# Query, output and key-sum transposition in a fused attention and two-layer feed-forward kernel: DMA in place of TensorE

## The chip, the cores and the metric

The kernel runs on one core of one Trainium2 chip. The metric is the device time of the whole program in microseconds (us). Engines are called by the names of the profile: PE is TensorE (matmuls), DVE is VectorE, ACT is ScalarE, POOL is GpSimd, and SP is SyncE, which issues every DMA of this kernel on one queue.

## The reference, cut to what matters

```python
# q (2, 12288, 128), kv (2, 384, 32, 128); the rows of q are scaled by 8
kv_pool = kv.reshape(B, H // 4, 4, W // 4, 4, C).mean(axis=(2, 4))   # 96 x 8 = 768 keys of 128
k = v = kv_pool.reshape(B, -1, C) @ w_sr
a = softmax((q @ k.transpose(0, 2, 1)) / sqrt(C))
x = (a @ v).reshape(B * S, D)                       # 24576 tokens of 128
h = x @ w_in;  x = (h * clip(h + 3, 0, 6) / 6) @ w_out        # d_ff = 2048
h = x @ w_in2; x = (h * cos(h)) @ w_out2                      # d_ff = 2048
```

## The kernel before

The tokens go in 48 blocks of 512, 24 for each of the two batches. In a block everything stands with the features on the partitions and the tokens along the row, so queries have to be transposed on the way in and outputs on the way out.

**Keys.** `plan_kv` (one call for each batch) makes the 768 pooled keys in six chunks of 128. A chunk is 16 rows of 128 features that have to be summed: two loads bring eight of them each, in two tiles of 128 x 1024. In the first batch (at the start of the program) the chunk is halved twice by adds of one half to the other (L448, `KV_HALVINGS` = 2), and the four parts that are left are summed and transposed by four PE matmuls against the identity (L457). In the second batch (in the middle of the program, beside other work) it is halved four times, in widths of 1024, 512, 256 and 128, and one PE matmul turns the result. Every add but the first has both operands in one SBUF tile; the first may go to DVE or to POOL.

**Attention.** `plan_attention` loads the block's queries (L550), turns them with four PE transposes of 128 x 128 into a PSUM bank (L558), and splits them into a high part (ACT, L561) and a low part (DVE, L564) in a tile x. Scores are L600, row maximum L606, exponential L612, normalisation on POOL L627. The attention weights are turned by a DMA: DVE lays the upper and lower half words of every value apart (L655), SP stores them to a DRAM scratch (L662), and a transposing DMA brings them back (L698); L714 multiplies them with the values (fp32 matmuls). Blocks 0 and 1 (`BY_PE` = 2) do that on PE instead (L683).

**Feed-forward.** `plan_unit` takes 256 hidden features: six matmuls of 512 columns in (L765 to L767), the gate on ACT and DVE (L780 and L783 in layer 1; L788, L791, L797, L800 in layer 2), a high part on ACT (L827), a low part on POOL (L803), and six matmuls out (L773 to L775). A block has 8 units in each layer. `plan_store` scales the result (ACT L850 or DVE L852), turns it by four PE transposes (L860), copies it out of PSUM (L325 on ACT, L327 on DVE) and stores it (L863).

**What sets the order.** Nothing is scheduled while it runs. `Plan.run` is a list scheduler that runs when the program is written: each step has a priority (`prio`, in nanoseconds), the engines it may use with an assumed cost, the steps it waits for, and the buffers it takes and gives back (13 tiles w of 128 x 1024 fp32, 7 hi, 6 lo, 6 x, 8 PSUM banks). It writes each engine's instructions in the order that it finds, and on the chip each engine goes through its row in that order, waiting where an operand is not there. A DMA takes a w tile only where more than `SPARE` = 5 are free.

## Time and profile before

| | us |
|---|---|
| three runs before, median (lowest to highest) | 2714.81 (2714.35 to 2715.35) |
| the profiled execution, its own time | 2709.69 |
| its span, first to last instruction | 2707.6 |
| PE busy in the span | 2641.4 |
| ACT busy | 2310.1 |
| DVE busy | 2115.5 |
| POOL busy | 2010.5 |

The views used are the page's busy times, a table of busy times by stretch of the span, the waits of one engine in one stretch, the timeline of one engine (start, duration, and in brackets the idle time before and what ended it), and the groups of instructions by line. The duration of a matmul overlaps the next one's, so its price is read from the distance of starts, not from its own length. The granted clock is given as a share of the upper of TensorE's two levels (1.2 and 2.4 GHz).

### The profile page before, as it was taken

Reading aid. Unit: us, or ns where it says so; the run is one execution under the profiler, and the core shown is the slowest. Engines: PE = TensorE matmul, PEld = TensorE weight load, DVE = VectorE, ACT = ScalarE, POOL = GpSimd, SP = SyncE. Lnnn points to the kernel's source line nnn. Section 1 sums busy time; section 2 is a strip of 40 time slices with the busy share of each in tenths; the row PEclk is TensorE's granted clock in tenths of the full one; section 3 lists DMA queues with packets and bytes.
Section 4 is the critical chain, followed back from the end, with each engine's and each line's share of the span. In section 5 each row is a group of like instructions: output and inputs, shape, how many; then the busy total and the mean of one; then the engine's idle time right before and its main releaser. Section 6 shows DMA issues by size and latency. Waiting matters only on the chain. (4 is left out here: it accounts for less than half of the span.)

```text
span 2707.6 us, 32274 instructions
## 1 busy us (share of the span) xinstructions
PE 2641.4 (98%) x11504; PEld 2100.2 (78%) x11504; DVE 2115.5 (78%) x2254; ACT 2310.1 (85%) x2647; POOL 2010.5 (74%) x969
## 2 busy tenths in 40 slices
PE   6889999999999999999999999999999999999999
PEld 5667877788878877778877888788878887888787
DVE  6998777777777887787777777777777777777776
ACT  4788889898988878888888888888888888989888
POOL 1657777777777777777777777777777777777777
PEclk9999999999999999999999999999999999999999
DMA  5422223222322243322232223222322232223210
GB/s 149 132 55 63 55 78 78 63 55 73 84 63 55 82 111 81 90 59 55 72 84 63 55 72 84 62 55 68 89 62 55 73 84 63 55 72 84 55 51 12
DMA packets 387056, 192.99 MB, mean 71 GB/s; under 512 B 292560, under 2 KB 367440, under 8 KB 386896
## 3 DMA queue, kind: packets, MB, share of 16 engines
q1 hardware_dynamic: 386896, 190.95, 27.1%
q8 instruction: 90, 1.47, 0.2%
q14 instruction: 70, 0.57, 0.1%
HBM read 33.62 MB, written 84.93 MB: 44 GB/s over the span
## 5 line engine op out<-in xcount | busy, mean ns | idle before, releaser
L803 POOL TENSOR_TENSOR lo<-w,hi 128x1024 fp32r<-128x1024 f32 x768 | 1834.7, 2412 | 635.3 <-ACT hi L827 387.8
L827 ACT CAST hi<-w 128x1024 fp32r<-128x1024 f32 x768 | 787.3, 1055 | 138.3 <-DVE w L783 79.2
L765 PE MATMUL banks<-x,w_in_hi 128*128 128x512 f32 x1536 | 636.3, 414 | 17.3 <-DVE w L783 9.7
L800 DVE TENSOR_TENSOR w<-w,banks 128x1024 f32<-128x1024 f32 x384 | 463.6, 1217 | 198.9 <-ACT w L797 198.6
L773 PE MATMUL banks<-hi,w_out_hi 128*128 128x512 f32 x1536 | 610.7, 398 | 7.2 <-DVE w L783 7.2
L774 PE MATMUL banks<-hi,w_out_lo 128*128 128x512 f32 x1536 | 600.7, 391 | 3.3 <-DVE w_out_lo L399 3.3
L775 PE MATMUL banks<-lo,w_out_hi 128*128 128x512 f32 x1536 | 600.9, 391 | 1.9 <-POOL lo L803 1.9
L767 PE MATMUL banks<-x,w_in_hi 128*128 128x512 f32 x1536 | 601.3, 391 | 0.1
L766 PE MATMUL banks<-x,w_in_lo 128*128 128x512 f32 x1536 | 600.8, 391 | 0.3
L783 DVE SCALAR_TENSOR_TENSOR w<-w,banks 128x1024 f32<-128x1024 f32 x384 | 457.8, 1214 | 116.9 <-ACT w L780 116.1
L791 DVE SCALAR_TENSOR_TENSOR w<-banks,w 128x1024 f32<-128x1024 f32 x384 | 463.7, 1217 | 60.1 <-ACT w L788 58.1
L780 ACT ACTIVATE w<-banks,three 128x1024 f32<-128x1024 f32 x384 | 418.1, 1115 | 55.8 <-PE banks L767 52.6
L788 ACT ACTIVATE w<-banks 128x1024 int32<-128x1024 f32 x384 | 389.0, 1026 | 56.1 <-PE banks L767 54.8
L797 ACT ACTIVATE w<-w 128x1024 f32<-128x1024 f32 x384 | 404.4, 1067 | 35.8 <-DVE w L791 33.1
L765 PEld LDWEIGHTS banks<-x,w_in_hi 128*128 128x128 f32 x1536 | 289.2, 188 | 115.3 <-DVE w L783 21.3
L766 PEld LDWEIGHTS banks<-x,w_in_lo 128*128 128x128 f32 x1536 | 289.5, 188 | 71.1 <-issue 15.1
L773 PEld LDWEIGHTS banks<-hi,w_out_hi 128*128 128x128 f32 x1536 | 289.5, 188 | 69.0 <-DVE w L783 8.1
L774 PEld LDWEIGHTS banks<-hi,w_out_lo 128*128 128x128 f32 x1536 | 289.6, 189 | 65.1 <-DVE w_out_lo L399 4.4
L775 PEld LDWEIGHTS banks<-lo,w_out_hi 128*128 128x128 f32 x1536 | 289.2, 188 | 63.9 <-POOL lo L803 2.8
L767 PEld LDWEIGHTS banks<-x,w_in_hi 128*128 128x128 f32 x1536 | 288.9, 188 | 62.7 <-DVE x L737 0.7
L655 DVE COPY w<-w 128x1536 uint16<-128x1536 uint16 x184 | 317.1, 1744 | 5.7 <-POOL w L627 5.1
L714 PE MATMUL banks<-w,v_all 128*128 128x512 f32 x576 | 269.6, 592 | 0.0
(64 smaller groups left out, 1915.5 us busy)
## 6 DMA issues: line engine op xcount, KB each, us to landing
scr<-w SPq DMA_DIRECT2D x184, 384.0 KB, 2.5
w<-in_kv_dram SPq DMA_DIRECT2D x48, 256.0 KB, 5.1
w<-in_q_dram SPq DMA_DIRECT2D x48, 256.0 KB, 2.8
out_dram<-w SPq DMA_DIRECT2D x48, 256.0 KB, 2.0
w<-in_moe_w_in_dram SPq DMA_DIRECT2D x8, 512.0 KB, 7.5
w<-in_moe_w_out_dram SPq DMA_DIRECT2D x8, 512.0 KB, 6.7
w<-scr SPq DMA_TRANSPOSE x138, 4.6
w_sr_sb<-in_w_sr_dram SPq DMA_DIRECT2D x1, 64.0 KB, 1.8
```

The lines of the kernel that those rows point to most:

```text
L765: nc.tensor.matmul(t[:, i, :], w_hi[:, k, :], xx[:, 0, :], start=True, stop=False)
L766: nc.tensor.matmul(t[:, i, :], w_lo[:, k, :], xx[:, 0, :], start=False, stop=False)
L767: nc.tensor.matmul(t[:, i, :], w_hi[:, k, :], xx[:, 1, :], start=False, stop=True)
L773: nc.tensor.matmul(t, o_hi[:, k, :], h[:, i, :], start=(k == 0), stop=False)
L774: nc.tensor.matmul(t, o_lo[:, k, :], h[:, i, :], start=False, stop=False)
L775: nc.tensor.matmul(t, o_hi[:, k, :], l[:, i, :], start=False, stop=(k == 2 * NP - 1))
L780: nc.scalar.activation(plan[g], two(ps), AF.Relu, bias=three, scale=1.0)
L783: nc.vector.scalar_tensor_tensor(out=plan[g], in0=plan[g], scalar=6.0, in1=two(ps), op0=ALU.min, op1=ALU.mult)
L791: nc.vector.scalar_tensor_tensor(out=plan[g], in0=two(ps), scalar=0.25, in1=plan[g].bitcast(I32), op0=ALU.add, op1=ALU.subtract,)
L800: nc.vector.tensor_tensor(out=plan[g], in0=plan[g], in1=two(ps), op=ALU.mult)
L803: nc.gpsimd.tensor_tensor(out=plan[lo], in0=plan[g], in1=plan[hi].bitcast(F32), op=ALU.subtract)
L827: prio + HI_AT, {"act": 947}, lambda e: nc.scalar.copy(plan[hi], plan[g]), [a],
```

## The change

Three things change.

1. **Queries** of blocks 2 to 47: the four PE transposes and the DVE subtraction go. Instead POOL lays the half words apart (L576), SP stores them to a new scratch `scrq` (L582), a transposing DMA brings them back into the same tile (L588), ACT makes the high part from SBUF (L594), and POOL the low part (L597). The load is planned 20 us earlier (`Q_AHEAD`).
2. **Outputs** of blocks 0 to 46: the four PE transposes and the copy out of PSUM go. POOL lays the half words apart (L917), SP stores them (L923), a transposing DMA brings them back (L928), and SP stores the result (L933).
3. **Key sums**, both batches: each half chunk of 128 x 1024 is summed by one DVE reduction over its eight rows (L449) into a small tile `sum`, reading with a step of one row (512 bytes), and two PE matmuls add the two halves and turn them (L458).

```diff
-KV_HALVINGS = 2
+Q_AHEAD = 20000
...
-            def add(n):
+            def add(half):
                 def emit(e):
-                    f, f2 = (flat(plan[k]) for k in keys) if n == 0 else (flat(plan[keys[0]]),) * 2
-                    w = 1024 >> n
-                    at = w if n else 0
-                    ENG[e].tensor_tensor(
-                        out=f[:, 0:w], in0=f[:, 0:w], in1=f2[:, at : at + w], op=ALU.add
-                    )
+                    f = flat(plan[keys[half]])
+                    nc.vector.tensor_reduce(
+                        out=plan[sums][:, half, :], in_=f.rearrange("p (x c) -> p c x", c=C),
+                        axis=AX.X, op=ALU.add,
+                    )
...
-                where = {"dve": 70 + (1.6 if b else 1.04) * w}
-                if n == 0:
-                    where["pool"] = 2303
-                a = [op(prio, where, add(n), a, drop=[] if n else [keys[1]])]
-            a = op(prio, {"pe": 216 * left}, transpose, a, take=[(ps, "one")],
+                a = op(
+                    prio, {"dve": 1135}, add(half), [load(half), a],
+                    take=[] if half else [(sums, "sum")], drop=[keys[half]],
+                )
+            a = op(prio, {"pe": 432}, transpose, [a], take=[(ps, "one")], drop=[sums])
...
-        a = op(prio + Q_AT, {"pe": 436}, transpose, [a], take=[(ps, "one")], drop=[raw])
-        a = op(prio + Q_AT + 100, {"act": 478}, high, [a], take=[(qt, "x")])
-        q_op = op(prio + Q_AT + 200, {"dve": 602}, low, [a], drop=[ps])
+            at = prio - Q_AHEAD
+            a = op(at - LOAD_AHEAD, {"dma": 1000}, load, take=[(raw, "w")])
+            a = op(at, {"pool": 1250}, halves, [a], take=[(scr, "scrq")])
+            a = op(at + 1000, {"dma": 500}, away, [a])
+            a = op(at + 2000, {"dma": 1500}, back, [a], drop=[scr])
+            a = op(prio + Q_AT + 100, {"act": 478}, high_t, [a], take=[(qt, "x")])
+            q_op = op(prio + Q_AT + 200, {"pool": 1230}, low_t, [a], drop=[raw])
...
         a = op(prio, {"act": 478, "dve": 600}, scaled, [after], take=[(o, "w")], drop=[acc])
+        if b < NB - 1:
+            a = op(prio + 2000, {"pool": 1250}, halves, [a], take=[(scr, "scro")])
+            a = op(prio + 2100, {"dma": 500}, away, [a])
+            a = op(prio + 2200, {"dma": 1500}, back, [a], drop=[scr])
+            op(prio + 2300, {"dma": 1000}, store_t, [a], drop=[o])
+            return
```

The new `halves`, `away` and `back` of a query block, which those of an output block follow with other shapes:

```python
def halves(e):    # 128 x 1024 half words, read with a step of two half words
    nc.gpsimd.tensor_copy(planes.rearrange("p (j h c) -> p j h c", j=NJ, h=2),
                          words.rearrange("p (j c h) -> p j h c", j=NJ, h=2))
def away(e):      # SP, SBUF to DRAM scratch
    nc.sync.dma_start(out=plan[scr].rearrange("(j p h) c -> p j (h c)", j=NJ, h=2), in_=parted()[1]...)
def back(e):      # SP, transposing DMA, DRAM scratch to SBUF
    nc.sync.dma_start_transpose(out=parted()[0], in_=plan[scr])
```

What that makes of the engines' rows is shown at three places. First PE, late in the second batch, where an output is turned between the value matmuls of a block (L714 before, L756 after). Before:

```order
L767 MATMUL banks<-x_107,w_in_hi 128x512
L714 MATMUL banks<-w_78,v_all 128x512 x2
L860 MATMUL banks<-ident,w_88 128x128 x4
L714 MATMUL banks<-w_89,v_all 128x512 x2
L765 MATMUL banks<-x_107,w_in_hi 128x512
L766 MATMUL banks<-x_107,w_in_lo 128x512
```

At the same place after (L807 to L809 are the former L765 to L767):

```order
L809 MATMUL banks<-x_104,w_in_hi 128x512
L756 MATMUL banks<-w_88,v_all 128x512 x2
L807 MATMUL banks<-x_104,w_in_hi 128x512
L808 MATMUL banks<-x_104,w_in_lo 128x512
L809 MATMUL banks<-x_104,w_in_hi 128x512
```

The four transposes are gone from the row, and what follows a value matmul is a feed-forward matmul; the query's four (L558) are missing in the same way a few rows on.

Second SP, one block's DMAs in the second batch (scr is the scratch of the attention weights, in_q the queries). Before:

```order
L698 DMA_TRANSPOSE w_90<-scr_120 128x2x1024
L863 DMA out_dram<-w_83 128x512
L550 DMA w_86<-in_q_dram 128x512
L662 DMA scr_118<-w_78 128x3x512
L662 DMA scr_118<-w_88 128x3x512
L662 DMA scr_118<-w_82 128x3x512
L662 DMA scr_118<-w_90 128x3x512
```

After:

```order
L549 DMA w_79<-in_q_dram 128x512
L740 DMA_TRANSPOSE w_89<-scr_128 128x2x1024
L740 DMA_TRANSPOSE w_88<-scr_128 128x2x1024
L740 DMA_TRANSPOSE w_81<-scr_128 128x2x1024
L923 DMA scro_124<-w_85 128x1024
L928 DMA_TRANSPOSE w_85<-scro_124 128x4x256
L582 DMA scrq_122<-w_79 128x4x256
L933 DMA out_dram<-w_85 128x512
L588 DMA_TRANSPOSE w_79<-scrq_122 128x1024
L704 DMA scr_128<-w_82 128x3x512
```

Two DMAs of a block between the attention's transposes and its stores have become five in a row, each of which waits for the one before it of its own chain; the query load has moved ahead of the attention's transposes.

Third DVE, the first chunk of the second batch's keys. Before:

```order
L448 TENSOR_TENSOR w_90<-w_90,w_81 128x1024
L564 TENSOR_TENSOR x_104<-banks,x_104 128x512
L791 SCALAR_TENSOR_TENSOR w_82<-banks,w_82 128x1024
L448 TENSOR_TENSOR w_90<-w_90 128x512
L783 SCALAR_TENSOR_TENSOR w_78<-w_78,banks 128x1024
L800 TENSOR_TENSOR w_82<-w_82,banks 128x1024
L783 SCALAR_TENSOR_TENSOR w_88<-w_88,banks 128x1024
L448 TENSOR_TENSOR w_90<-w_90 128x256
L448 TENSOR_TENSOR w_90<-w_90 128x128
```

After (L833 and L842 are the former L791 and L800):

```order
L449 TENSOR_REDUCE sum_110<-w_88 128x128
L842 TENSOR_TENSOR w_83<-w_83,banks 128x1024
L833 SCALAR_TENSOR_TENSOR w_84<-banks,w_84 128x1024
L833 SCALAR_TENSOR_TENSOR w_87<-banks,w_87 128x1024
L842 TENSOR_TENSOR w_84<-w_84,banks 128x1024
L842 TENSOR_TENSOR w_87<-w_87,banks 128x1024
L833 SCALAR_TENSOR_TENSOR w_82<-banks,w_82 128x1024
L449 TENSOR_REDUCE sum_110<-w_90 128x128
```

Four adds whose two operands lie in SBUF have become two reductions with one operand, and the gate's steps stand between them.

## Rows read from the trace of the kernel before

**Rows 1.** The page's busy times of the engines, with their share and instruction counts.

```profile
PE 2641.4 (98%) x11504; PEld 2100.2 (78%) x11504; DVE 2115.5 (78%) x2254; ACT 2310.1 (85%) x2647; POOL 2010.5 (74%) x969
```

**Rows 2.** Busy time by stretch of the span; the first line names the columns.

```profile
core 0: us, PE busy (x) PEld busy (x) DVE busy (x) ACT busy (x) POOL busy (x), PEclk, DMA share, GB/s
0.00:57.00 57.00, 35.87 (x201) 29.58 (x202) 32.53 (x56) 20.22 (x39) 7.88 (x15) 1.00 0.63 176
57.00:212.00 155.00, 134.68 (x543) 98.63 (x541) 145.53 (x185) 124.87 (x148) 90.31 (x43) 0.98 0.30 84
212.00:940.00 728.00, 727.48 (x3180) 581.80 (x3179) 564.77 (x601) 636.29 (x725) 564.25 (x273) 1.00 0.26 67
940.00:1170.00 230.00, 211.39 (x893) 165.45 (x892) 192.85 (x182) 183.85 (x210) 164.65 (x76) 0.97 0.35 90
1170.00:2600.00 1430.00, 1429.44 (x6251) 1143.37 (x6250) 1106.86 (x1169) 1252.26 (x1428) 1097.88 (x530) 1.00 0.26 68
```

**Rows 3.** Waits of PE from 940 to 1170 us: total, times, longest.

```profile
PE banks L457 <- DVE w L448: 6.4, 2, 3.3
PE banks L773 <- DVE w L783: 5.8, 1, 5.8
```

**Rows 4.** Timeline of PE around a query's four transposes: start, duration, instruction.

```profile
1004.80 0.40 PE L775 MATMUL banks<-lo,w_out_hi 128*128 128x512 f32 x1
1005.04 0.60 PE L558 MATMUL banks<-ident,w 128*128 128x128 f32 x4
1005.39 0.48 PE L765 MATMUL banks<-x,w_in_hi 128*128 128x512 f32 x1
1005.71 0.40 PE L766 MATMUL banks<-x,w_in_lo 128*128 128x512 f32 x1
1005.94 0.40 PE L767 MATMUL banks<-x,w_in_hi 128*128 128x512 f32 x1
```

**Rows 5.** Groups by line: the PE transposes of outputs and of queries.

```profile
L860 PE MATMUL banks<-ident,w 128*128 128x128 f32 x192 | 28.8, 273 | 0.7 <-ACT w L850 0.7
L558 PE MATMUL banks<-ident,w 128*128 128x128 f32 x192 | 28.6, 272 | 1.4 <-DVE x L741 1.4
```

**Rows 6.** Timelines of DVE, POOL and PE in the second batch's key sums.

```profile
1036.71 7.35 DVE L448 TENSOR_TENSOR w<-w 128x512 f32<-128x512 f32 x3
...
1036.27 7.64 POOL L803 TENSOR_TENSOR lo<-w,hi 128x1024 fp32r<-128x1024 f32 x3 [0.66 <-ACT hi L827]
...
1045.25 0.79 PE L773 MATMUL banks<-hi,w_out_hi 128*128 128x512 f32 x1 [5.77 <-DVE w L783]
...
1172.37 0.28 DVE L448 TENSOR_TENSOR w<-w 128x128 f32<-128x128 f32 x1
```

**Rows 7.** Groups by line (count, busy us, mean ns, idle before), and one line's shortest/median/longest.

```profile
L803 POOL TENSOR_TENSOR lo<-w,hi 128x1024 fp32r<-128x1024 f32 x768 | 1834.7, 2412 | 635.3 <-ACT hi L827 387.8 <-PE banks L775 124.6 <-issue 84.5
L627 POOL TENSOR_SCALAR w<-w,s 128x768 f32<-128x768 f32 x192 | 174.6, 921 | 55.0 <-DVE s L623 48.4 <-ACT w L612 2.8 <-DMA w<-in_moe_w_out_dram 2.3
L606 DVE TENSOR_REDUCE s<-banks 128x1 f32<-128x768 f32 x192 | 179.8, 953 | 82.2 <-PE banks L600 78.9
...
L655 DVE COPY w<-w x184: 1731/1744/1756, 93.7 to 2595.4; 128x1536 uint16<-128x1536 uint16 x184
```

**Rows 8.** Timelines of DVE and PE at the first batch's last chunk of keys.

```profile
28.02 1.23 DVE L448 TENSOR_TENSOR w<-w,w 128x1024 f32<-128x1024 f32 x1 [1.97 <-DMA w<-in_kv_dram]
29.28 0.69 DVE L448 TENSOR_TENSOR w<-w 128x512 f32<-128x512 f32 x1
...
30.12 1.13 PE L457 MATMUL banks<-ident,w 128*128 128x128 f32 x8 [2.12 <-DVE w L448]
```

**Rows 9.** DMA issues by line: count, KB each, median us from issue to landing.

```profile
scr<-w SPq DMA_DIRECT2D x184, 384.0 KB, 2.5
w<-in_q_dram SPq DMA_DIRECT2D x48, 256.0 KB, 2.8
w<-scr SPq DMA_TRANSPOSE x138, 4.6
```

More of the change, by code (lines that the diff above doesn't have):

```diff
@@ L296, in attention_ffn_ffn_kernel @@
             "x": tiles("x", NX, [P, 2, T], F32R),
+            "sum": tiles("sum", 2, [P, 2, C], F32),
             "s": tiles("s", 8, [P, 4], F32),
@@ L454, in transpose @@
             def transpose(e):
-                for i in range(left):
-                    f = flat(plan[keys[i // 8]])
+                for i in range(2):
                     nc.tensor.matmul(
-                        one(ps)[:, 0:P], f[:, i % 8 * C : (i % 8 + 1) * C], ident,
-                        start=(i == 0), stop=(i == left - 1),
+                        one(ps)[:, 0:P], plan[sums][:, i, :], ident,
+                        start=(i == 0), stop=(i == 1),
                     )
@@ L567, in low, with parted, halves, turned @@
             )
-        a = op(prio - LOAD_AHEAD, {"dma": 1000}, load, take=[(raw, "w")])
-        a = op(prio + Q_AT, {"pe": 436}, transpose, [a], take=[(ps, "one")], drop=[raw])
-        a = op(prio + Q_AT + 100, {"act": 478}, high, [a], take=[(qt, "x")])
-        q_op = op(prio + Q_AT + 200, {"dve": 602}, low, [a], drop=[ps])
+        scr = ("scrq", b)
+        def parted():
+            t = flat(plan[raw]).bitcast(U16)
+            return t[:, 0 : 2 * T], t[:, 2 * T : 4 * T]
+        def halves(e):
+            words, planes = parted()
+            nc.gpsimd.tensor_copy(
+                planes.rearrange("p (j h c) -> p j h c", j=NJ, h=2),
+                words.rearrange("p (j c h) -> p j h c", j=NJ, h=2),
+            )
+        def away(e):
+            nc.sync.dma_start(
+                out=plan[scr].rearrange("(j p h) c -> p j (h c)", j=NJ, h=2),
+                in_=parted()[1].rearrange("p (j x) -> p j x", j=NJ),
+            )
+        def back(e):
+            nc.sync.dma_start_transpose(out=parted()[0], in_=plan[scr])
+        def turned():
+            return flat(plan[raw])[:, 0:T]
+        def high_t(e):
+            nc.scalar.copy(plan[qt][:, 0, :], turned())
+        def low_t(e):
+            nc.gpsimd.tensor_tensor(
+                out=plan[qt][:, 1, :], in0=turned(), in1=plan[qt][:, 0, :].bitcast(F32),
+                op=ALU.subtract,
+            )
+        if b < BY_PE:
+            a = op(prio - LOAD_AHEAD, {"dma": 1000}, load, take=[(raw, "w")])
+            a = op(prio + Q_AT, {"pe": 436}, transpose, [a], take=[(ps, "one")], drop=[raw])
+            a = op(prio + Q_AT + 100, {"act": 478}, high, [a], take=[(qt, "x")])
+            q_op = op(prio + Q_AT + 200, {"dve": 602}, low, [a], drop=[ps])
+        else:
+            at = prio - Q_AHEAD
[5 more added lines that the diff above has]
+            q_op = op(prio + Q_AT + 200, {"pool": 1230}, low_t, [a], drop=[raw])
         scaled, first = [], None
@@ L865, in store, with parted, halves, away @@
             )
-        a = op(prio, {"act": 478, "dve": 600}, scaled, [after], take=[(o, "w")], drop=[acc])
+        scr = ("scro", b)
+        def parted():
+            t = flat(plan[o]).bitcast(U16)
+            return t[:, 0 : 2 * T], t[:, 2 * T : 4 * T]
+        def halves(e):
+            words, planes = parted()
+            nc.gpsimd.tensor_copy(
+                planes.rearrange("p (h q) -> p h q", h=2),
+                words.rearrange("p (q h) -> p h q", h=2),
+            )
+        def away(e):
+            nc.sync.dma_start(
+                out=plan[scr].rearrange("(c h) q -> c (h q)", h=2), in_=parted()[1],
+            )
+        def back(e):
+            nc.sync.dma_start_transpose(
+                out=parted()[0].rearrange("p (j x) -> p j x", j=NJ), in_=plan[scr]
+            )
+        def store_t(e):
+            nc.sync.dma_start(
+                out=rows(out, b), in_=plan[o][:, 0, :].rearrange("p (j c) -> p j c", c=C)
+            )
+        a = op(prio, {"act": 478, "dve": 600}, scaled, [after], take=[(o, "w")], drop=[acc])
+        if b < NB - 1:
[4 more added lines that the diff above has]
+            return
         a = op(prio + 2000, {"pe": 436}, transpose, [a], take=[(ps, "one")])
@@ L898, in pool_kv @@
     def pool_kv(prio, batch):
-        step, *how = (KV_STEP, 4, 0) if batch else (2000, KV_HALVINGS, WARM)
-        projects[batch] = plan_kv(prio, batch, step, *how)
+        projects[batch] = plan_kv(prio, batch, *((KV_STEP, 0) if batch else (2000, WARM)))
     def project_kv(prio, batch):
```

13 lines of the change are left out of this document (6 added, 7 removed).

## The prediction

> **What bounds the kernel now.** I read the page's busy times first: PE is busy for 98% of the span and the next engine, ACT, for 85% [rows 1]. Such a share can hide idle stretches, so the second view is the table by stretch [rows 2]. The reader is to see two things in it. From 212 to 940 us and from 1170 to 2600 us PE is busy for 727.48 of 728 and for 1429.44 of 1430 us: there the program is as long as PE's own work, and nothing else counts. In three stretches PE is idle: 21.1 us at the start (0 to 57), 20.3 us from 57 to 212, and 18.6 us from 940 to 1170. In the last one the granted clock is 0.97 as well, where it is 1.00 in the saturated ones: of 211 us of work about 3%, some 6 us, are lost beside the idle time, so that stretch gives away about 25 us. The third view says what it waits for there: DVE, by name the key sums (L448, 6.4 us) and a gate step (L783, 5.8 us at once) [rows 3]. The timelines join the two: from 1036.71 DVE spends 7.35 us on three adds of 512, 256 and 128 columns, exactly as long as three L803 keep POOL busy (7.64 us from 1036.27); the gate step stands behind them in DVE's row, and PE's wait of 5.77 us ends with it. With POOL idle, the narrowest of these adds takes 0.28 us [rows 6]. So an add with two operands in SBUF waits for POOL here.
>
> **Part 1, the PE transposes.** 46 query blocks and 47 output blocks lose four transposes each. The price is read from starts: from the last matmul before (1004.80) to the second after (1005.71) are 0.91 us, and without the four there would be two steps of 0.23 us, as from 1005.71 to 1005.94 [rows 4]. That is 0.45 us a set; I take 0.44, since starts are rounded. Outputs and queries have the same shape and the same mean (273 and 272 ns) [rows 5]. PE is the limit where nearly all of them stand, so 93 x 0.44 = **-41 us**, all of it on the path. ACT loses a copy and DVE a subtraction for a block; neither is the bound, worth nothing.
>
> **Part 2, what takes their place.** On POOL two copies of 128 x 1024 half words and one subtraction of 512 columns for a block. The subtraction is half an L803, 1.21 us. A POOL copy of half words is not in the trace: the nearest rows are L627, one operand, 921 ns for 768, so 1.23 us for 1024, and L803, two operands, 2.41 us [rows 7]. I take 1.23, since one operand is read; both ends stay in the range. So 3.7 us for a block. In the stretch to 2600 POOL has 530 instructions, 20 a block (16 L803, 4 L627), so it is 26.5 blocks of 54.0 us with 41.4 us of POOL work each [rows 2]; after it is 45.1 of about 53.1 us, 85% (with copies of 2.41 us 89%). The cover is POOL's own idle time, 635 us before L803, most of it waiting for ACT's high part [rows 7]; where that cover is gone, L803 comes late and the matmuls out wait. On SP four more DMAs for a block, each chain waiting for the landing before it. Behind a waiting one in SP's row stand the others: the store waits for L928, the query's return stands behind the store, and the next block's L704 behind that, whose transposes feed PE. A query's chain is 2.8 (load) + 1.23 + 2.5 (a store, as scr<-w, which is larger) + between 2.3 and 4.6 (half of a 4.6 us transpose, or all of its latency) [rows 9], plus up to 7.2 us behind three L803: 9 to 18 us, against the 24 us (`LOAD_AHEAD` 5 + `Q_AHEAD` 20 - 1) by which its load is now planned ahead. A w tile is held some 20 us longer for a query and some 6 us for an output, 0.5 tile of 13 on average. I cost all this at nothing in the steady part, because DMAs, POOL and tiles have the cover named, but not in the first 212 us, where PE is idle for 41 us already, or wherever an assumed cost is off in the new order: **+5 us**, a quarter of the idle time from 57 to 212; bounds 0 and the whole 41.
>
> **Part 3, the key sums.** A reduction of 1024 elements is not in the trace with its operand in SBUF. L606 reduces 768 in 953 ns, 1.24 ns each, so 1.27 us for 1024. It would not wait for POOL as the adds do: L655, the DVE operation that reads and writes SBUF with one operand, lies between 1731 and 1756 ns in all 184 cases, beside POOL or not [rows 7]. So a chunk of the second batch costs 2.5 us of DVE in place of four adds of which three alone took 7.35 us, and the waits of [rows 3] go with them. Of the 25 us I take back 20, leaving 5 for the waits that a shifted order makes anew: **-20 us**; bounds 0 and -25. PE has two matmuls a chunk there instead of one, two records of a quarter of 0.44 us: 6 x 0.22 = **+1.3 us**. At the start, loads set the pace (DVE waits 1.97 us for the last chunk's DMA at 28.02). After it come an add of 1.23, one of 0.69, then eight matmul records until about 31.1 us [rows 8]; now one reduction of 1.27 and half the records: 0.65 + 0.45 = **-1.1 us**.
>
> One rule of the Trainium skill speaks for this and one against. "SBUF — State Buffer", section "Who interferes with whom", says that a DVE instruction with two SBUF inputs contends with GpSimd and a `tensor_reduce` never does; the trace agrees as to the adds (0.28 us alone, 7.35 us for three beside POOL). The same page, section "Door 1: The DMA port swizzle", says that each access to a new 16-byte line of SBUF pays a penalty, and here every read is a row of 512 bytes on. No run here shows a read of such a step; the rival "slow sums" below prices it.
>
> **Sum.** -41 - 20 + 1.3 - 1.1 + 5 = -55.8 us. The profiled execution took 2709.69 us (span 2707.6), which becomes 2654 us. It lies 5.1 us under the median of the runs; from the median, 2714.8 - 55.8 = **2659 us**.
>
> **The rivals.**
> *Slow sums.* The stepped read doubles a reduction to 2.5 us. Then the second batch needs 5 us of DVE a chunk, its waits stay (+20), and at the start twelve reductions take 30 us and no longer fit between the loads (+7): 2659 + 27 = **2686 us**. For it: no row shows such a read. Against: L655 with a step of two half words runs at 1.14 ns an element, hardly less than the 1.24 of the row-wise L606.
> *Given back.* POOL at 85% or SP's chained DMAs come late now and then, 0.3 to 1 us a block: +14 to +46, **2673 to 2705 us**, middle 2689. At the upper end it looks like no change. For it: L803 waits 388 us for ACT, so POOL's idle time isn't free to choose. Against: in the stretch to 2600 PE is idle for 0.6 us in all, for POOL or anything else [rows 2].
> *Slower: queries come late.* L597 now stands in POOL's row among the L803, and SP's L588 behind the output's chain; if the scores (L642) wait for them, PE stands still, since its row is fixed, and the exponentials behind them too. The price is that wait, once a block. It decides at 55.8 / 46 = 1.2 us a block; at 2 us it is 2659 + 92 = **2751 us**. For it: two more engines stand on the query's way. Against: 24 us of lead for a chain of 9 to 18.
> A POOL copy would have to take (54.0 - 41.4 - 1.2) / 2 = 5.7 us for POOL to become as long as the block was before; more than twice L803, so I count it under this one.
>
> **How the numbers follow.** Forecast 0.62, with its own range of 2649 (nothing new, all 25 us back) to 2674 (15 us more of new waits); slow sums 0.15; given back 0.15, a fifth of it within 0.2% of before; queries late 0.08. A measurement of this kernel can tell about 0.2%, here 5.4 us. So faster 0.62 + 0.15 + 0.12 = 0.89, same 0.03, slower 0.08. The range goes from 2647 to 2692: nearly all of the forecast, most of the slow sums, and half of what is given back, 0.8 in all.
>
> **What would show it.** In the profile after, PE should stay at 98% or more with some 41 us less work, and the stretches from 212 to 940 and from 1170 on without idle time. L449 near 1.27 us right through, also beside POOL, and no wait of PE for it in the middle confirm part 3; 2 us or more in an idle stretch is the slow sums. L576 and L917 near 1.23 us confirm POOL's price. I am wrong if L642 waits for POOL, if L756 waits for a DMA (SP held up), or if L817 waits for L845 block after block.

## The result and the profile after

| | before | after |
|---|---|---|
| runs, median (lowest to highest), us | 2714.89 (2714.35 to 2715.35) | 2669.11 (2667.97 to 2672.55) |
| ratio, with its 95% interval | | 0.9834 [0.9817, 0.9851] |
| the profiled execution, us (span) | 2709.69 (2707.6) | 2667.97 (2666.2) |

The change saves 45.8 us between the medians, against the 55.8 forecast: 2669 instead of 2659, inside the range. A second set of runs gave 2672.46 against 2712.99, 0.9853 [0.9836, 0.9869].

The lines move by 42 for most of the kernel: L765 to L767 are now L807 to L809, L773 to L775 are L815 to L817, L783 is L825, L800 is L842, L803 is L845, L827 is L869, L600 is L642, L612 is L654, L714 is L756. The page's busy times of after, to hold against [rows 1]:

```profile
PE 2613.4 (98%) x11120; PEld 2064.6 (77%) x11120; DVE 2089.0 (78%) x2185; ACT 2299.1 (86%) x2613; POOL 2152.9 (81%) x1106
```

PE is busy for 28 us less, where the prediction asked for some 41, and POOL for 142 more. The page counts a matmul of 512 columns as 0.39 us long though the next one starts 0.23 us later, so a step that comes up to 0.16 us late still counts as busy: the busy time is not the work. Busy time by stretch, for [rows 2]: the span and the busy time (count) of PE, PEld, DVE, ACT and POOL, then the granted clock.

```profile
0.00:57.00 57.00, 40.60 (x188) 32.90 (x189) 44.66 (x58) 20.69 (x42) 11.18 (x18) 1.00 0.64 190
57.00:212.00 155.00, 134.21 (x518) 99.83 (x517) 147.05 (x188) 126.00 (x148) 98.74 (x49) 0.93 0.36 92
212.00:940.00 728.00, 726.17 (x3107) 576.26 (x3106) 563.00 (x584) 643.37 (x727) 614.11 (x316) 1.00 0.36 90
940.00:1170.00 230.00, 227.99 (x979) 179.94 (x978) 192.96 (x189) 197.32 (x226) 187.40 (x96) 1.00 0.47 115
1170.00:2560.00 1390.00, 1385.15 (x5911) 1096.84 (x5911) 1072.36 (x1110) 1225.22 (x1384) 1158.85 (x593) 1.00 0.35 87
```

The middle is where the eye goes first: from 940 to 1170 us PE was busy for 211.39 us at a clock of 0.97 and is now busy for 227.99 at 1.00. Its waits there, for [rows 3], no longer have the sums' name:

```profile
PE banks L807 <- DVE w L825: 1.0, 1, 1.0
PE banks L807 <- DVE w L842: 0.5, 2, 0.3
PE banks L807 <- ACT w L654: 0.3, 1, 0.3
```

The long stretches say the opposite, and more quietly: PE's idle time rose from 0.5 to 1.8 us (212 to 940), and is 4.9 us from 1170 to 2560 where it had been 0.6; 1.9 of the 4.9 are one wait for L825 at 1238.84. The new instructions, for [rows 7], first the groups of POOL with busy us, mean ns and idle time before:

```profile
L597 POOL TENSOR_TENSOR x<-w,x 128x512 fp32r<-128x512 f32 x46 | 59.9, 1302 | 5.5 <-ACT x L594 5.5
L917 POOL COPY w<-w 128x1024 uint16<-128x1024 uint16 x47 | 49.0, 1042 | 10.7 <-DVE w L894 10.6
L576 POOL COPY w<-w 128x1024 uint16<-128x1024 uint16 x46 | 47.9, 1042 | 26.8 <-DVE sum L449 26.8
```

And the reductions, with shortest, median and longest in ns:

```profile
L449 DVE TENSOR_REDUCE sum<-w x24: 1866/1948/2073, 5.8 to 1131.3; 128x128 f32<-128x1024 f32 x24
```

The copies are cheaper than forecast (1.04 us, not 1.23), the subtraction a little dearer (1.30, not 1.21), and the reductions much dearer: 1.95 us, not 1.27.

To see where the time went, the two PE timelines are laid side by side by work done, not by time. A block has 96 matmuls out (six for each of 16 units). The start of the last of these is taken as the block's end. At such a mark two kernels have not always done the same other work: at the end of block 2 the kernel with the lead of 8 us (below) has 18 matmuls in fewer behind it than the kernel before, and at the end of block 16 the changed kernel has 6 matmuls in and 12 records of value matmuls more. Each is put right at its price in starts (0.227 us for a matmul in, 0.43 for a record of a value matmul); the transposes are what the change takes away and are not put right. Each column then shows how much earlier (negative) a stretch of blocks ran than in the kernel before, at equal work. The forecast's column puts its terms where they belong: 0.88 us a block for two sets of transposes, the sums in the middle, +5 and -1.1 at the start. The second execution is that of the second set of runs. The last column is a later experiment on the same chip, the same change with the queries planned 8 us ahead instead of 20.

| stretch, to the end of block | forecast | after | after, second execution | lead of 8 us |
|---|---|---|---|---|
| 2 (start) | +3.9 | -0.6 | +3.9 | +4.9 |
| 16 | -12.3 | -7.1 | -7.2 | -9.7 |
| 27 (holds the second batch's key sums) | -28.4 | -26.1 | -26.0 | -27.9 |
| 42 | -13.2 | -6.6 | -6.6 | -10.0 |
| 48 | -5.3 | -2.1 | -2.2 | -3.2 |
| sum | -55.3 | -42.5 | -38.2 | -46.0 |

The middle is within 2.3 us of the forecast. The saturated stretches on both sides of it are not: they should have run 25.5 us faster and ran 13.6, and the two executions agree there. They differ at the start, by 4.5 us. From block 27 to 42 the two ends are these rows of the PE timelines, of before and of after (the work between them is the same but for the transposes):

```profile
1586.91 0.39 PE L775 MATMUL banks<-lo,w_out_hi 128*128 128x512 f32 x1
...
2396.59 0.39 PE L775 MATMUL banks<-lo,w_out_hi 128*128 128x512 f32 x1
```

```profile
1557.91 0.39 PE L817 MATMUL banks<-lo,w_out_hi 128*128 128x512 f32 x1
...
2361.04 0.39 PE L817 MATMUL banks<-lo,w_out_hi 128*128 128x512 f32 x1
```

Fifteen blocks take 809.68 us before and 803.13 after: 53.98 and 53.54 us a block. So 0.44 us a block is gained, where the transposes that left are worth 0.88. Half of it came back. This is the part of the loss that the view names as waits, in the PE timeline of after (start, duration, instruction, and in brackets the idle time before and what ended it):

```profile
1405.59 0.40 PE L809 MATMUL banks<-x,w_in_hi 128*128 128x512 f32 x1
1406.28 0.50 PE L807 MATMUL banks<-x,w_in_hi 128*128 128x512 f32 x1 [0.29 <-DVE w L825]
1406.62 0.40 PE L808 MATMUL banks<-x,w_in_lo 128*128 128x512 f32 x1
...
1407.56 0.39 PE L809 MATMUL banks<-x,w_in_hi 128*128 128x512 f32 x1
1408.22 0.50 PE L815 MATMUL banks<-hi,w_out_hi 128*128 128x512 f32 x1 [0.27 <-DVE w L825]
```

From start to start the two steps take 0.69 and 0.66 us instead of 0.23. Here PE's row has matmuls in of several units of layer 1 behind each other, 1.36 us for a unit. ACT, which has to read each unit out of PSUM (L822) and round it (L869), turns to the next one every 1.95 us, and DVE's gate L825 follows ACT. These are ACT's rows at that place:

```profile
1401.90 1.12 ACT L822 ACTIVATE w<-banks,three 128x1024 f32<-128x1024 f32 x1 [0.29 <-PE banks L809]
1402.91 1.04 ACT L869 CAST hi<-w 128x1024 fp32r<-128x1024 f32 x1
1403.86 1.11 ACT L822 ACTIVATE w<-banks,three 128x1024 f32<-128x1024 f32 x1
1404.86 1.04 ACT L869 CAST hi<-w 128x1024 fp32r<-128x1024 f32 x1
1405.80 1.12 ACT L822 ACTIVATE w<-banks,three 128x1024 f32<-128x1024 f32 x1
```

The unit's PSUM banks come free with L825, so after a few units PE waits for banks. None of the new instructions stands in this chain. The pattern comes back every five blocks. With the steps of 0.34 us behind them the two waits cost some 1.1 us, so 0.2 of the 0.44 us a block; the other half lies in steps that come late by too little for the view to call it a wait.

PE's row shows when this happens. A run here is a number of units whose matmuls in follow each other with no other work of PE between. From 1330 to 2560 us it has 14 runs of six units, and all ten waits that the view has there (five of L807, five of L815) belong to five of these runs, one before the last unit and one right behind it. In the fifteen blocks from 28 to 42 the kernel before has no run of more than three units.

### The profile page after: what moved, and what is told of

Read it like the earlier page. It is cut to its first block, busy times and chain, and to the rows that moved or that the text cites. A ratio compares the mean times of both kernels' runs of the same rounds, so it can differ in the third digit from the quotient of the medians.

```text
span 2666.2 us, 32082 instructions
## 1 busy us (share of the span) xinstructions
PE 2613.4 (98%) x11120; PEld 2064.6 (77%) x11120; DVE 2089.0 (78%) x2185; ACT 2299.1 (86%) x2613; POOL 2152.9 (81%) x1106
## 5 line engine op out<-in xcount | busy, mean ns | idle before, releaser
L845 POOL TENSOR_TENSOR lo<-w,hi 128x1024 fp32r<-128x1024 f32 x768 | 1835.9, 2409 | 418.1 <-ACT hi L869 233.0
L869 ACT CAST hi<-w 128x1024 fp32r<-128x1024 f32 x768 | 793.2, 1051 | 111.3 <-DVE w L842 75.8
L807 PE MATMUL banks<-x,w_in_hi 128*128 128x512 f32 x1536 | 635.4, 414 | 19.5 <-DVE w L842 7.3
L815 PE MATMUL banks<-hi,w_out_hi 128*128 128x512 f32 x1536 | 629.5, 410 | 2.7 <-DVE w L825 2.3
L809 PE MATMUL banks<-x,w_in_hi 128*128 128x512 f32 x1536 | 603.1, 393 | 1.4 <-DVE x L779 1.4
L817 PE MATMUL banks<-lo,w_out_hi 128*128 128x512 f32 x1536 | 600.8, 391 | 2.2 <-POOL lo L845 2.2
L842 DVE TENSOR_TENSOR w<-w,banks 128x1024 f32<-128x1024 f32 x384 | 465.2, 1217 | 143.9 <-ACT w L839 143.4
L825 DVE SCALAR_TENSOR_TENSOR w<-w,banks 128x1024 f32<-128x1024 f32 x384 | 462.6, 1216 | 117.3 <-ACT w L822 116.7
L833 DVE SCALAR_TENSOR_TENSOR w<-banks,w 128x1024 f32<-128x1024 f32 x384 | 466.0, 1219 | 108.4 <-ACT w L830 106.9
L822 ACT ACTIVATE w<-banks,three 128x1024 f32<-128x1024 f32 x384 | 423.6, 1118 | 43.3 <-PE banks L809 38.9
L839 ACT ACTIVATE w<-w 128x1024 f32<-128x1024 f32 x384 | 404.9, 1062 | 57.5 <-DVE w L833 55.3
L830 ACT ACTIVATE w<-banks 128x1024 int32<-128x1024 f32 x384 | 390.5, 1024 | 55.9 <-PE banks L809 53.5
L807 PEld LDWEIGHTS banks<-x,w_in_hi 128*128 128x128 f32 x1536 | 290.0, 189 | 119.4 <-DVE w L825 25.9
L815 PEld LDWEIGHTS banks<-hi,w_out_hi 128*128 128x128 f32 x1536 | 288.8, 188 | 79.0 <-issue 10.5
L809 PEld LDWEIGHTS banks<-x,w_in_hi 128*128 128x128 f32 x1536 | 289.8, 189 | 64.8 <-DVE x L779 1.8
L817 PEld LDWEIGHTS banks<-lo,w_out_hi 128*128 128x128 f32 x1536 | 288.4, 188 | 64.8 <-POOL lo L845 3.4
L756 PE MATMUL banks<-w,v_all 128*128 128x512 f32 x576 | 270.7, 593 | 0.0
```

The lines of the kernel that those rows point to most:

```text
L807: nc.tensor.matmul(t[:, i, :], w_hi[:, k, :], xx[:, 0, :], start=True, stop=False)
L809: nc.tensor.matmul(t[:, i, :], w_hi[:, k, :], xx[:, 1, :], start=False, stop=True)
L815: nc.tensor.matmul(t, o_hi[:, k, :], h[:, i, :], start=(k == 0), stop=False)
L817: nc.tensor.matmul(t, o_hi[:, k, :], l[:, i, :], start=False, stop=(k == 2 * NP - 1))
L822: nc.scalar.activation(plan[g], two(ps), AF.Relu, bias=three, scale=1.0)
L825: nc.vector.scalar_tensor_tensor(out=plan[g], in0=plan[g], scalar=6.0, in1=two(ps), op0=ALU.min, op1=ALU.mult)
```

## The experiments

**One part at a time.** Four kernels on one chip, where the one before took 2711.82 us: the queries alone, the outputs alone, the sums alone, and queries and outputs together with the old sums.

Queries alone (outputs by PE and the old sums put back):

```diff
-        if b < NB - 1:
+        if False:
             a = op(prio + 2000, {"pool": 1250}, halves, [a], take=[(scr, "scro")])
```

> Only the queries go by the transposing DMA; outputs and key sums as before. Theory A (the removed transposes are worth 0.44 us each, and about half comes back as short waits of TensorE for the gate, because the matmuls in now come faster than ACT and VectorE free the PSUM pairs): 46 x 0.44 = 20 us less, 0 to 10 given back, 2695 to 2705 us. Rival B (what comes back is GpSimd's load: this is the part with the larger load, a copy of 1.04 and a subtraction of 1.30 us a block): more comes back here than with the outputs alone, 2703 us or more, and the steady blocks show TensorE waiting for L845 or L597.

Measured: 2691.60 us, 0.9926 [0.9912, 0.9941], or 20.2 us less, below the 2695 to 2705 of theory A and far from rival B. The total is the price of the 46 sets nearly to the point, but by luck: by stretches, as in the table, it is +2.0, -2.2, -13.1 in the middle (with the old sums, where 11 sets are worth 4.8), -3.9 for the fifteen blocks to 42, or 0.26 us a block instead of 0.44, and -1.3.

Outputs alone (queries by PE and the old sums put back):

```diff
-        if b < BY_PE:
+        if True:
             a = op(prio - LOAD_AHEAD, {"dma": 1000}, load, take=[(raw, "w")])
```

> Only the outputs go by the transposing DMA. Theory A: as for the queries, 47 x 0.44 = 21 us less, 0 to 10 given back, 2694 to 2704 us. Rival B: GpSimd has only one copy of 1.04 us a block more, so next to nothing comes back, 2694 us, clearly less than with the queries alone.

Measured: 2712.64 us, 1.0006 [0.9996, 1.0015]: nothing, against the 2694 to 2704 of both theories. 47 sets of transposes have left PE's row, worth 20 us by their own length, and the blocks from 27 to 42 take 53.96 us each, as before. PE's waits for gates in the whole span (total, times, longest), first of the kernel before, then of this one:

```profile
PE banks L765 <- DVE w L783: 9.7, 9, 3.5
PE banks L773 <- DVE w L783: 7.2, 2, 5.8
PE banks L765 <- DVE w L800: 6.3, 5, 2.4
PE banks L600 <- DVE w L783: 1.8, 1, 1.8
```

```profile
PE banks L809 <- DVE w L827: 13.4, 16, 3.5
PE banks L809 <- DVE w L844: 10.6, 7, 3.1
PE banks L644 <- DVE w L827: 6.9, 2, 4.4
PE banks L817 <- DVE w L827: 5.6, 10, 1.5
```

(L827 is L825 of after, L844 its L842.) All are gates, as in the full change. They rose from 25.0 to 36.5 us, by about half of the 20; the rest is in no wait that the view names. From 1330 us on this kernel's row has six runs of seven units of matmuls in, each with one wait in it and one right behind it. POOL has only one copy a block more in this kernel, 1.04 us, less than in any other kernel with transposes removed, yet all of the gain is gone. That speaks against POOL's load as the cause.

Sums alone (queries and outputs by PE):

```diff
-        if b < BY_PE:
+        if True:
             a = op(prio - LOAD_AHEAD, {"dma": 1000}, load, take=[(raw, "w")])
...
-        if b < NB - 1:
+        if False:
             a = op(prio + 2000, {"pool": 1250}, halves, [a], take=[(scr, "scro")])
```

> Only the key sums are changed. Theory A (the waits of 940 to 1170 us came from the two-operand adds behind GpSimd): idle time and the lower clock of that stretch go, 25 us, and 2 us at the start: 2688 us. Rival (the stretch recovered because the transposes and the query subtraction left it room): less than 12 us, 2703 us or more, and TensorE idle for over 8 us from 940 to 1170.

Measured: 2693.61 us, 0.9934 [0.9919, 0.9949], or 18.2 us less, 5 us short of theory A (2688) and clear of the rival. By blocks it is the cleanest of all: +2.3 us at the end of block 2 and still +2.3 at 16, -16.1 at 27, and -16.1 to the end. The sums act in the middle and nowhere else, there by 18.4 us. From 940 to 1170 PE is busy for 226.54 us at 1.00 in this kernel.

Queries and outputs with the old sums:

```diff
-        projects[batch] = plan_kv(prio, batch, *((KV_STEP, 0) if batch else (2000, WARM)))
+        step, *how = (KV_STEP, 4, 0) if batch else (2000, 2, WARM)
+        projects[batch] = plan_kv(prio, batch, step, *how)
```

> The changed kernel with the key sums as they were before. Theory A: the parts add up, 2669 + 27 = 2696 us, with the waits for the adds back in the middle. Rival (GpSimd's higher load stretches the adds further): over 2702 us, adds of 512 columns and less of more than 2 us on the mean.

Measured: 2677.35 us, 0.9873 [0.9856, 0.9889], or 34.5 us less, a better time than both theories gave. Waits are back in the middle, though fewer than before (11.8 us of PE idle instead of 18.6); they have the names of gates, which stand behind the adds in DVE's row. PE's waits from 940 to 1170:

```profile
PE banks L645 <- DVE w L828: 6.6, 2, 5.1
PE banks L810 <- DVE w L845: 3.8, 2, 2.2
```

And DVE's timeline in that stretch, where an add of 256 columns takes 1.78 us and one of 128 takes 1.47:

```profile
1034.07 1.78 DVE L450 TENSOR_TENSOR w<-w 128x256 f32<-128x256 f32 x1
1035.78 2.67 DVE L651 TENSOR_REDUCE s<-banks 128x1 f32<-128x768 f32 x3
1038.37 1.47 DVE L450 TENSOR_TENSOR w<-w 128x128 f32<-128x128 f32 x1
```

Each of these two adds ends within 0.3 us of a POOL operation beside it. With the sums alone changed the waits go, so the adds did cause them. The four runs together show that the parts do not add up: 20.2 and -0.8 make 19.4 for queries and outputs apart, and together they give 34.5. The sums, worth 18.4 us in the middle alone, add 9.1 there to the other two (17.0 with the old sums, 26.1 with the new). A sum in which each part has a price of its own misses something that depends on the whole.

**The price of the reduction.** Why 1.95 us and not 1.27? The reduction reads its elements 512 bytes apart. One kernel lets it read them in a row.

```diff
-                        out=plan[sums][:, half, :], in_=f.rearrange("p (x c) -> p c x", c=C),
+                        out=plan[sums][:, half, :], in_=f.rearrange("p (c x) -> p c x", c=C),
```

> The changed kernel, but each key-sum reduction (L449) adds eight neighbouring features of one row instead of the same feature of eight rows, so its sums are wrong; its reads then follow each other without a step. Everything else, the order of every row too, is the same. Theory (the step of 512 bytes is what makes the reduction dear): L449 falls from a median of 1.95 us to 1.27 (1024 elements at the 1.24 ns of L606). At the start ten reductions stand back to back, so the first projection matmul comes up to 10 x 0.68 = 6.8 us earlier, or less where loads then set the pace: 0.9835 of before goes to 0.981 to 0.983, 2 to 6.8 us less than the changed kernel. In the middle nothing changes, because no PE wait there has the sums' name any more. Rival (the 1.95 us is the price of a reduction whose operand is in SBUF, whatever the step): L449 stays at 1.9 us and the time at 0.9834 of before.

Measured: 2666.05 us, 0.9828 [0.9813, 0.9842]. The reductions (shortest, median, longest, all 24):

```profile
L449 DVE TENSOR_REDUCE sum<-w x24: 1208/1220/1221, 5.8 to 1131.6; 128x128 f32<-128x1024 f32 x24
```

And the middle stretch (span, then busy time of PE and the others):

```profile
940.00:1170.00 230.00, 230.00 (x997) 183.84 (x996) 187.60 (x192) 200.63 (x229) 191.33 (x98) 1.00 0.50 120
```

The step is the price: 1.22 us in a row, 1.95 us with it, 60% more. 1.22 is the row-wise price of the forecast (1.27) nearly to the point. The whole time cannot be told from that of the changed kernel, 0.9828 against 0.9834 and 0.9853. By stretches it can: the order of the rows is the same, and the middle gains 31.1 us here against 26.1 and 26.0 in the changed kernel and 27.1 in the next experiment. So the step costs 4 to 5 us there, against the expectation that the middle would not change: 2.0 of it are the idle time that is gone from 940 to 1170 us. At the start the shorter reductions simply wait for their loads (14.2 us in 11 waits).

**POOL's cover.** Each new POOL copy is issued twice, in the same order of rows.

```diff
+            for _ in range(2):
-            nc.gpsimd.tensor_copy(
+                nc.gpsimd.tensor_copy(
```

> The changed kernel, but each of the POOL copies that lay half words apart (L576, L917) is issued twice, with the second writing the same values again; the order of all rows is the same. That is 93 x 1.04 = 97 us more of POOL, 2.08 us a block. Theory (POOL's own idle time covers the replacement work; the waits that came back are a matter of the order of the rows): the time rises by 0 to 8 us, 0.983 to 0.987 of before, and the waits of PE for the gate (L825) stay at about the same sum. Rival (POOL's load is what gives back 17 us: 3.3 us of it a block did that): 2.08 us more should give back another 17 x 2.08 / 3.3 = 11 us or more, 0.9875 of before or above, with L817 waiting for L845.

Measured: 2673.09 us, 0.9852 [0.9835, 0.9868]; the changed kernel itself has 0.9834 and, in its second set of runs, 0.9853. POOL is busy for 2247.1 us instead of 2152.9. The fifteen blocks from 27 to 42 take 53.54 us each, the same as in the changed kernel. The groups of POOL:

```profile
L919 POOL COPY w<-w 128x1024 uint16<-128x1024 uint16 x94 | 98.0, 1042 | 6.3 <-DVE w L895 2.6
L577 POOL COPY w<-w 128x1024 uint16<-128x1024 uint16 x92 | 95.7, 1040 | 32.7 <-DMA w<-in_q_dram 29.9
```

And PE's waits, of which L826 is the gate and L846 the former L845:

```profile
PE banks L808 <- DVE w L826: 6.4, 13, 1.9
...
PE banks L818 <- POOL lo L846: 3.2, 2, 2.5
PE banks L816 <- DVE w L826: 2.8, 9, 0.5
```

94 us more of POOL work cost nothing in a steady block. So the load of these copies gives nothing back there.

**The order alone.** If no instruction has a price that explains the loss, the order is left. Two kernels hold the same instructions as the changed one; only the number by which the list scheduler plans a query's chain ahead differs, and so the order that it finds.

```diff
-Q_AHEAD = 20000
+Q_AHEAD = 8000
```

(16000 in the other.)

> The changed kernel with the queries' chain planned 8 us ahead instead of 20. The same instructions, the same operands; only the list scheduler finds another order, and a query holds its w tile 12 us less. Theory (the 17 to 20 us that came back are a chance of the order, not a price of any new instruction): the time moves by 4 to 15 us, in either direction, and it moves with the sum of PE's waits for the gates (L825, L842) in the steady part, while L642 goes on waiting for no query; earlier release of tiles rather makes it faster, 0.978 to 0.982 of before. Rival (queries late): the chain of load 2.8, copy 1.0, store 2.3 and return 3.1, 9.2 us plus waits in POOL's and SP's rows, no longer fits in 8 + 5 - 1 = 12 us, and L642 waits about 1 us a block for POOL's L597: +46 us, 1.000 of before.

> The changed kernel with the queries' chain planned 16 us ahead instead of 20: same instructions, an order of rows that differs, 4 us less of holding a w tile for each query. Theory (chance of the order): the time moves by more than 4 us although the lead hardly changes, by my reading upwards, to 0.985 to 0.992 of before, by waits of the feed-forward matmuls for gates. Rival (the held tile, or the length of the lead, is what costs): the time lies between that of the changed kernel and that of the lead of 8 us, a third of the way.

Measured: 2664.66 us, 0.9823 [0.9808, 0.9837], with 8 us, and 2677.60 us, 0.9869 [0.9855, 0.9884], with 16 us, on one chip. The same work in three orders: 0.9823, 0.9834 to 0.9853, 0.9869. From 27 to 42 the blocks take 53.33 us with the lead of 8 and 53.32 with that of 16, against 53.54 with 20. PE from 1330 to 2560 us, first the changed kernel, then the one with the lead of 8 us (in its second set of runs):

```profile
1330.00:2560.00 1230.00, 1227.09 (x5238) 971.98 (x5237) 953.27 (x985) 1086.59 (x1225) 1029.73 (x526) 1.00 0.36 88
```

```profile
1330.00:2560.00 1230.00, 1230.00 (x5263) 975.53 (x5262) 948.69 (x990) 1077.24 (x1219) 1029.61 (x527) 1.00 0.35 88
```

With the lead of 8 us no idle time of PE is left there, and the waits for the gate are gone from the view. So are the long runs: from 1330 us on its row has none of more than three units of matmuls in. With the lead of 16 us there are three of six, the last at 1520 us, one of them with two waits, and after it none. The rival for the lead of 16 us, that the time a query holds its tile is the price, falls: the steady blocks are as fast as with 8, and what that kernel loses against it (12.4 us by the end) it has lost nearly all by the end of block 2, where at equal work it is 16.8 us behind the kernel before and the lead of 8 us 5.1. Half of my expectation for the lead of 16 us was right (slower), but not by the waits that I named. Neither lead makes queries late: L642 does not wait for L597 in either.

**What the start loses.** At the end of block 8 the kernel with the lead of 8 us is 4.8 us behind the kernel before and not 5 ahead. That reading, by which the two expectations below go, does not allow for the work that has moved across the mark. At equal work the two kernels are level there: +5.1 at the end of block 2, then -5.1 to the end of block 8, where the forecast has -5.3. So what there is to explain is the start. Two kernels on one chip (before: 2710.39 us) build on that kernel: one turns the queries of blocks 2 to 5 by PE, one makes the first batch's sums as before.

```diff
-        if b < BY_PE:
+        if b < 6:
             a = op(prio - LOAD_AHEAD, {"dma": 1000}, load, take=[(raw, "w")])
```

> The kernel with the lead of 8 us, but with the queries of blocks 2 to 5 turned by PE as in the kernel before; blocks 6 to 47 by DMA. It tests what the start loses: with the lead of 8 us the steady blocks gain 0.65 us each, yet at the end of block 8 the kernel is 4.8 us behind the one before instead of 5 us ahead, so some 8 to 10 us go in the first 500 us. Theory 1 (the query chains of the first blocks collide there with the loads and splits of the weights and with the idle clock): 4 to 8 us come back, less 4 x 0.35 us for the transposes, 2658 to 2661 us or 0.980 to 0.981 of before. Theory 2 (those blocks lose the time by the gates' and exponentials' order, whoever turns the queries): the time stays within 3 us of that of the lead of 8 us, 0.9815 to 0.9835.

```diff
-            a = None
-            for half in range(2):
+            if b == 0:
+                a = [load(0), load(1)]
+                for n in range(halvings):
...
+            else:
+                a = None
+                for half in range(2):
```

> The kernel with the lead of 8 us, but with the first batch's key sums made as in the kernel before (two adds and four matmuls a chunk); the second batch's sums stay reductions. Theory 1 (reductions of 1.95 us, twelve in a row, are the pace of the start, and the adds did as well or better): the first projection matmul is not later than with the reductions, the waits for the sums at the start stay at 13 to 18 us in all, and the time stays within 3 us of that of the lead of 8 us, 0.9815 to 0.9835 of before. Theory 2 (the forecast's: fewer records and no second add bring 1.1 us at the start): the time rises by 1 to 3 us. Rival (the sums are what the first 500 us lose): the time falls by 4 us or more, 0.981 or less.

Measured: 2661.29 us, 0.9818 [0.9801, 0.9834], and 2663.16 us, 0.9823 [0.9809, 0.9838]. Neither can be told from the lead of 8 us by these intervals. With the old sums PE waits for them for 19.2 us at the start, more than the 13 to 18 expected and than the 14.8 of the reductions, and the end of block 2 comes at the same time (+4.9 us at equal work in both). So the first batch's sums, fast or slow, are worth nothing that shows. With the queries by PE the start is +2.4, 2.5 us less, and the blocks 3 to 8 gain 5.4 us, hardly more than with the lead of 8 us. That is below the 4 to 8 us of the first theory, within what two executions of one kernel differ by at the start, and the whole run does not confirm it.

**The changed kernel and the lead of 8 us on one chip**, five rounds each (before: 2712.99 us).

> The changed kernel once more, beside the one with a lead of 8 us on the same chip. 0.982 to 0.985 of before.

> The kernel with the lead of 8 us once more, beside the changed one. Theory (steady blocks of 53.32 us against 53.54 for 21 blocks, less what start and middle take back): 3 to 6 us less than the changed kernel. Rival (the two differ by the chip and the run alone): within 1.5 us of it.

Measured: 2672.46 us (2670.64 to 2672.89), 0.9853 [0.9836, 0.9869], and 2663.14 us (2662.93 to 2664.11), 0.9821 [0.9806, 0.9835]. The lowest run of the one is 6.5 us above the highest of the other, and the medians are 9.3 us apart, more than the 3 to 6 that I expected. So the lead of 8 us beats both kernels: 49.9 us less than before. In the two profiled executions (spans 2670.5 and 2662.3) the table says where it lies: 2.5 us from block 2 to 16, 1.9 in the middle, 3.4 from 27 to 42, 1.0 behind them, and 1.0 the other way at the start.

## Why the prediction was right and where it was off

**The bound.** Right: PE is the busiest engine in every kernel here, with 97 to 98% of the span. That it had no room left between 1170 and 2600 us [rows 2] was read from a busy time that hides short delays. By starts, the blocks 28 to 42 of the kernel before hold 15 steps that are more than 0.03 us too long, 1.7 us in all, eight of them ended by the gate L800.

**Part 1, the transposes, -41 us.** The price of a set is right: with each kind of step of PE's row at its usual length from start to start, the fifteen blocks from 28 to 42 come to 804.1 us before and 791.1 after, 0.87 us a block. The step that failed is "all of it on the path", and with it the "nothing" that part 2 put down for the steady part. A block that loses 0.88 us of PE work ends 0.44 us earlier in the changed kernel, 0.67 in its best order, 0.26 with the queries alone (of 0.44), and no earlier with the outputs alone (of 0.44). What stands in its place is lateness of PE's steps: waits for gates, as shown above, for about half of it, and shorter delays for the rest. My reading, from the rows, is this: ACT needs 1.95 us for a unit whose matmuls in take PE 1.36, so PE outruns it wherever such units follow each other, and work of PE that stood between them was cover; how much of the cover is missed depends on the order. The runs show that the order decides, with the same instructions, and that from 1330 us on the waits belong to runs of six or seven units and are gone where no run is longer than three. No run changes ACT's pace alone, so the pace as the reason is argued and not shown.

**Part 2, what takes its place, 0 with +5 of new waits.** That POOL, SP and the tiles cost nothing was right as far as it was tried: PE does not wait for L597, L756 never waits for a DMA, L817 waits for L845 twice in the whole span, and doubling the copies changes no steady block. The chains land well within the lead (store 2.3 and return 3.1 us for queries), and even 8 us of lead suffice. The +5 is the term that was mis-sized. By the table it was about +18 in the first execution (42.5 gained of 60.3 without any new wait) and +22 in the second. At the start, where I put it, it was 0.5 in the one and 5.0 in the other; the other 17 lay behind the start, for which I had put nothing: 5.2 between blocks 2 and 16, 6.6 between 27 and 42, 3.2 behind them, and 2.3 in the middle. The rival "given back" came near in size (its lowest value is 2673 us, the two sets of runs gave 2669 and 2672) and had the wrong cause: it named POOL and SP, and the runs name the order of PE's row. The row that I held against it, 0.6 us of idle PE from 1170 to 2600 [rows 2], was true of the old order only.

**Part 3, the sums, -20 + 1.3 - 1.1.** Right for the sums alone, which give 18.4 us in the middle; their +2.3 at the start says little, since two executions of the changed kernel differ there by 4.5. In the change as a whole they give 9.1, half of that (6 to 11 by the medians of the whole runs), and the other two parts give 17.0 in the middle where 9.7 were forecast. So that the middle came out right is in part luck: the two errors cancel. Queries by DMA alone already gain 13.1 us there, of which their transposes are 4.8; why they take away so much of the waits for the old sums is not shown. The reduction's price was wrong: 1.95 us, nearer the 2.5 of the rival "slow sums" than the 1.27 of the forecast. But that rival's conclusion, that the waits then stay, was wrong too. What mattered most in the middle was not the length but that a reduction isn't held up by POOL as an add is: with a step it took 1.87 to 1.90 us at the start, where POOL is idle, and 2.00 to 2.07 in the middle beside it, and in a row 1.21 to 1.22 in all 24 cases, where adds of 512, 256 and 128 columns took 7.35 us together [rows 6]. A chunk thus costs some 4.1 us of DVE in the middle for certain, and DVE, 78% busy, has room for most of that: reductions of 1.22 us gain 4 to 5 us more there. This is what the Trainium skill's page "SBUF — State Buffer" says in "Who interferes with whom" (a `tensor_reduce` never contends with GpSimd). The trace agrees as to the row-wise reductions; what makes a stepped one 8% longer in the middle stays open. Its remark in "Door 1: The DMA port swizzle", that each access to a new 16-byte line pays a penalty, is borne out as well, with a size that it doesn't give: 1.95 against 1.22 us.

**Start.** Forecast +5 - 1.1, measured at equal work -0.6 to the end of block 2 in one execution and +3.9 in another of the same kernel, +5.1 and +4.9 with the lead of 8 us. The stretch from 57 to 212 us has less clock than before, 0.93 of the upper level instead of 0.98; from 150 to 190 us it is 0.85, where PE waits five times for 1.9 to 3.1 us, for L842 and L654. It is a few microseconds either way, and the executions differ by as much.

**What stays open.** Of the 0.88 us a block, 0.2 are missing even in the best order, 3.0 us in the fifteen blocks. Some 2.2 of these are spread over steps that are less than 0.03 us too long. Part of the rest can be read: in each block one score matmul (L642) starts 0.08 us late, and its weight load (PEld) waits for the gate L825, 34 times and for 6.3 us in the whole span. Open is also what makes the start of one kernel differ by 4.5 us between two executions, and why the order with the lead of 16 us loses 12 us more there.

## What to carry to other kernels

Work taken out of a saturated engine is worth its full length only where nothing else makes the engine late; here, with the next engine 85% busy, between a quarter and all of it came back. Look at the places where the engine would run ahead of the next one, not at the new instructions alone, and read starts, since a busy share of 98% hides short delays. In a kernel whose order is found by a list, measure the change in two or three orders before judging it: the same instructions lay 13 us apart here, and one number set anew was worth 9 us. When two timelines are compared at marks, check that the same work lies before the marks: here a loss of 4 us between blocks 2 and 8 was only work that had moved across them. An operation that is longer but is not held up by another engine can take the place of shorter ones that are.

## What the runs showed of the hardware that was not expected

- A DVE reduction of 1024 fp32 elements from SBUF takes 1.21 to 1.22 us when it reads them in a row, POOL busy beside it or not. With a step of 512 bytes it takes 1.87 to 1.90 us at the start, with POOL idle, and 2.00 to 2.07 in the middle of the program, beside POOL.
- A POOL copy of 1024 half words of each partition with a step of two takes 1.04 us, less than half of a two-operand POOL operation on 1024 fp32 elements (2.41 us).
- A DVE add with both operands in SBUF took 1.47 us for 128 columns beside POOL (with the old sums), where it takes 0.28 alone [rows 6].
- The 93 new transposing DMAs, of 256 KB each, landed 3.1 to 3.3 us after their issue, and those of the attention weights beside them took 4.8 us instead of 4.6 [rows 9].
